# GpSimd's elementwise work goes to VectorE, and elu gets another instruction mix

## The chip, the cores and the metric

One NeuronCore of a Trainium2 chip runs the whole program. The metric is device time in microseconds (us) for one execution. Three runs of the kernel before gave 858.94, 859.1 and 861.25 us, so the median is 859.1 us.

Five engines work side by side, each through its own queue in program order: TensorE (PE, with its weight loads as PEld), VectorE (DVE), ScalarE (ACT), GpSimd (POOL) and SyncE (SP), which issues transfers. An instruction that waits holds up everything behind it on its engine.

## The reference, cut to what matters

```python
x = attn_out.transpose(0, 2, 1, 3).reshape(2304, 512)    # masked attention, 4 x 8 heads, 576 rows
order = argsort(-(x @ w_gate).flatten())                 # each token gets one of 8 experts,
...                                                      # each expert takes at most 288 tokens
for e in range(8):
    out[assigned == e] = np.maximum(x[assigned == e] @ w1[e], 0.0) @ w2[e]
h = out @ w_in                                           # 512 -> 2048
g = np.where(h > 0.0, h, np.exp(np.minimum(h, 0.0)) - 1.0)   # elu
return g @ w_out                                         # 2048 -> 512
```

All of it is float32. To keep that accuracy at TensorE's fast rate, each matmul operand is split into a high part (a rounded copy) and a low part (the rest), and each product is made of three matmuls: high by high, high by low, low by high.

## The kernel before, in words

The program has two stretches. Up to about 108 us it computes attention, 24 steps of a software pipeline. Behind it, for each of the eight experts in turn (`expert`, L1186), it computes the expert's two layers for 288 tokens (`h_item`, `y_item`), and then the dense layer pair for the full 128-token chunks that are ready (`hin_item`, `elu`, `out_item`; 256 or 384 columns, 16 slices of the 2048 hidden units). Beside this run the routing of a later expert (`Router.phase`: a chain of small DVE instructions with a group of small matmuls between them, six digit steps per expert), the gather of its rows (`rows_of`, indirect DMAs issued by POOL) and the splitting of the weights:

- Expert weights arrive as `raw` (128x512). `feeder` (L979) has ACT make the high part `wh` (L997) and then has a subtraction make the low part `wl` (L220, in `Dense.tt`). It runs on POOL or DVE.
- Dense weights arrive as 64-bit words, and `Dense.slice` (L229) unpacks them during attention and the first expert: two ACT instructions (L245, L248), a shift and two merges on DVE (L251, L256), two multiplications `g` and, for most slices, an ACT copy (L282) and two subtractions (`dense_lo`, `parts`). Multiplications and subtractions are L220 again, on POOL or DVE.

`Line` is a planner that runs while the program is built. It keeps an estimated clock for each engine and decides in which order the instructions are written; nothing of it runs on the chip. `Line.either` (L179) picks the engine for L220, and the flag `quiet` keeps POOL out:

```python
if self.free['pool'] <= self.now + POOL_AHEAD and not self.quiet:
    return 'pool'
if self.idle('dve', 65 + 1.05 * n):
    return 'dve'
```

Before, `quiet` is set only in the last digit step of the first routing (L715) and while gathers are outstanding (`rows_of`, L1032 to L1044).

`elu` (L1126) takes a PSUM tile `h` (in two cases the tile `yo` of another pool) with the dense layer's sums: ACT writes exp(h) to the SBUF tile `e` (L1146), DVE clamps it to 1 and subtracts 1 in place (L1148), DVE takes the maximum with `h` (L1150), ACT copies the result to the high part `ah` (L1152), and DVE makes the low part `al` by subtraction (L1154). For an expert's first layer the pair is ACT `ah` (L1082) and DVE `al` (L1084). PSUM tiles `h` have three buffers. TensorE waits for `al` and `wl` before the matmuls that read them.

Of the kernel before, what the change touches and what calls it, by code (L numbers as in the profile page):

```python
# [10 lines left out]
F32 = mybir.dt.float32  # L11
# [4 lines left out]
AF = mybir.ActivationFunctionType  # L16
OP = mybir.AluOpType
# [4 lines left out]
B, H, S, D = 4, 8, 576, 64  # L22
# [4 lines left out]
NS = len(BITS)  # L27
# [562 lines left out]
class Router:  # L590
# [100 lines left out]
    def phase(self, p, res, bank, then=None):  # L691


        nc, t, line, n = self.nc, {k: x[:, :self.n] if k in COLUMNS else x for k, x in self.t.items()}, self.line, self.n
        v, D = nc.vector, line.dve
# [7 lines left out]
        def pe(m, cost):  # L703
# [2 lines left out]
            line.now += m * cost  # L706
            return line.now + line.LAT

        if p:
            yield from self.prelude(p, 0, n)  # L710
        if p < 7:
            parts = ((0, n),) if p else ((0, 10), (10, 18))
            for i in range(NS):
                K = 2 ** BITS[i] - 1
                line.quiet = line.hush = p == 0 and i == NS - 1  # L715
                e = []
                for c0, c1 in parts:
                    n1 = self.against(t['ohU'][:, c0:c1, :K + 1], t['cur'][:, c0:c1], 96, 97 + K, OP.is_ge)
                    e.append(D(n1, fast=2) + line.late())
                if i == 0:  # L720
                    for j in range(1, NS):
                        self.digit(j, 0, n)
                    v.tensor_copy(t['digf'][:, 1:, :n], t['dig'][:, 1:, :n])
                    D(n * NS)
                else:
                    v.tensor_copy(t['di'], t['d'])
                    D(1)
                if i < NS - 1:
                    v.scalar_tensor_tensor(t['cd'], t['cur'][:, :, 0], 64.0, t['digf'][:, i + 1, :n], op0=OP.mult, op1=OP.add)
                    D(n)  # L730
                if i == 1:
                    v.tensor_scalar(t['pre'], t['di'], SHIFT[0], None, op0=OP.logical_shift_left)
                elif i > 1:
                    v.scalar_tensor_tensor(t['pre'], t['di'], SHIFT[i - 1], t['pre'], op0=OP.logical_shift_left, op1=OP.bitwise_xor)
                D(1)
                if i == 2:
                    v.tensor_scalar(t['mk'], t['pre'], 31, -1, op0=OP.arith_shift_right, op1=OP.bitwise_xor)
                    D(1)
                elif i == 3:
                    v.scalar_tensor_tensor(t['pre'], t['mk'], -2 ** 31, t['pre'], op0=OP.bitwise_or, op1=OP.bitwise_xor)  # L740
                    D(1)
                yield e[0]
                pc = yield from bank.take("pc")
                for (c0, c1), x in zip(parts, e):
                    yield x
                    for c in range(c0, c1):
                        nc.tensor.matmul(pc[:, :K], t['oh'][:, c, :], t['ohU'][:, c, :K], start=(c == 0), stop=(c == n - 1))
                yield pe(n, 30) if p else line.now + (c1 - c0) * 40 + line.LAT
                v.tensor_scalar(t['ok'][:, :K], pc[:, :K], CAP - 0.5, 0.0, op0=OP.is_ge, op1=OP.add, accum_out=t['d8'])
                e = D(K)  # L750
                bank.free(e + line.late())
                yield e
                v.transpose(t['tr'], t['d8'].to_broadcast([128, 32]))
                yield D(32)
                v.tensor_reduce(t['d'], t['tr'][:, 0:8], axis=AX.X, op=OP.max)
                e = D(8)
                if i == NS - 1:
                    v.tensor_reduce(t['di'], t['tr'][:, 0:8], axis=AX.X, op=OP.max)
                    D(8)
                yield e  # L760
                if i < NS - 1:
                    v.scalar_tensor_tensor(t['cur'], t['d'][:, :, None].to_broadcast([128, n, 4]), -64.0, bc(t['cd'], 4), op0=OP.mult, op1=OP.add)
                    e = D(4 * n)
                v.scalar_tensor_tensor(t['q'], t['tr'][:, 0:8], t['d'], t['q'] if i else self.e8, op0=OP.is_equal, op1=OP.mult)
                e = max(e, D(8))
                if i == NS - 1:
                    v.tensor_tensor(t['T'].bitcast(I32), t['di'], t['pre'], op=OP.bitwise_xor)
                    D(1)
                yield e
            eqe = t['q']  # L770
        else:
            eqe = t['eqe']
            v.scalar_tensor_tensor(eqe, self.caps, 0.0, self.e8, op0=OP.is_gt, op1=OP.mult)
            v.memset(t['T'], -2 * BIG)
            yield D(8)
# [7 lines left out]
        e = D(n)  # L783
        v.scalar_tensor_tensor(eqt, t['m'], t['T'], t['inE'], op0=OP.is_equal, op1=OP.mult)
        h = D(n) + line.late()
# [15 lines left out]
        e = D(2 * n)  # L801
# [7 lines left out]
        e = D(4 * n)  # L809
        v.tensor_tensor(t['V'], bc(t['t12'], 3), rb(self.io3, n), op=OP.is_equal)  # L810
        f = D(3 * n)
        yield e
        e = []
        for c0, c1 in parts if p < 7 else ((0, n),):
            n1 = self.against(t['ohU'][:, c0:c1, :96], t['u'][:, c0:c1], 0, 96, OP.is_equal)
            e.append(((c0, c1), D(n1, fast=2) + line.late()))
        (v if p else nc.gpsimd).tensor_tensor(
            t['vp'].rearrange("p c (v k) -> p c v k", k=4), t['V'][:, :, :, None].to_broadcast([128, n, 3, 4]),
            self.tokp[:, :, None, :].to_broadcast([128, n, 3, 4]), op=OP.mult)
        yield D(12 * n) + line.late() if p else line.pool(216, f)  # L820
        pi = yield from bank.take("pi")
        for (c0, c1), x in e:
            yield x
# [4 lines left out]
        e = D(12)  # L828
# [99 lines left out]
class Moe:  # L928
# [92 lines left out]
    def rows_of(self, p, res):  # L1021
        nc, line = self.nc, self.line
        while 'idx' not in res:
            yield line.now + 40
        idx = res['idx']
        rows = self.one.tile([96, 3, DM], F32, name="rows")
        at = []
        for v in range(3):
            nc.gpsimd.indirect_dma_start(out=rows[:, v], out_offset=None, in_=self.x_d[:, :],
                                         in_offset=bass.IndirectOffsetOnAxis(ap=idx[:, v, 0:1], axis=0))  # L1030
            at.append(line.dma(196608, line.put('pool', 1030), False) + GATHER)
        line.quiet = True  # L1032
        if p == 0:
            self.warm(WARM)
        nc.sync.dma_start(self.ids[CAP * p:CAP * p + CAP].rearrange("(v u) o -> u (v o)", u=96), idx[:, :, 1])
        if p:
            yield at[2]
            line.quiet = False
        while self.stage1 < p - 1:
            yield line.now + 60  # L1040
        for v in range(3):
            yield at[v] + (ROWS_LATE if p else 0)
            if not p and v == 2:
                line.quiet = line.hush = False  # L1044
            if p:
                pt = yield from self.bank.take("px")
            else:
                pt = self.hp.tile([128, 512], F32, name="h")
            pt = pt[:, 0:384].rearrange("p (k u) -> p k u", k=4)
            for k in range(4):  # L1050
                nc.tensor.transpose(pt[:, k], rows[:, v, 128 * k:128 * k + 128], self.identf[0:96, 0:96])
            line.now += 4 * 92
            h, l = self.xh[:, :, 96 * v:96 * v + 96], self.xl[:, :, 96 * v:96 * v + 96]
            yield line.now + line.LAT
            nc.scalar.activation(h, pt, AF.Copy)
            yield line.act(384)
            nc.vector.tensor_tensor(l, pt, h.bitcast(F32), op=OP.subtract)
            self.x_at = line.dve(384)
            if p:
                self.bank.free(self.x_at + line.late())  # L1060
        self.x_for = p
# [64 lines left out]
    def elu(self, ph, N, spare=None, split=False):  # L1126
        nc, line = self.nc, self.line
# [9 lines left out]
        def evac(c0, c1, E):  # L1137
            yield line.now + line.LAT
            if not E:
                while self.open == 2:  # L1140
                    yield line.now + 20
                self.open += 1
                E.append(self.tmp.tile([128, 384], F32, name="e")[:, :N])
            e, x, h, l = (z[:, c0:c1] for z in (E[0], ph, gh, gl))
            n = c1 - c0
            nc.scalar.activation(e, x, AF.Exp)  # L1146
            yield line.act(n)
            nc.vector.tensor_scalar(e, e, 1.0, -1.0, op0=OP.min, op1=OP.add)  # L1148
            line.dve(n, fast=2)
            nc.vector.tensor_tensor(e, e, x, op=OP.max)  # L1150
            yield line.dve(n)
            nc.scalar.activation(h, e, AF.Copy)  # L1152
            yield line.act(n)
            nc.vector.tensor_tensor(l, e, h.bitcast(F32), op=OP.subtract)  # L1154
            A['t'][c0 // 128:c1 // 128] = [line.dve(n)] * (n // 128)
            self.open -= c1 == N

# [214 lines left out]
```

## Time and profile before

| What | Value |
|---|---|
| median of three runs | 859.1 us (858.94 to 861.25) |
| the profiled execution's own time | 863.49 us |
| its span, first to last instruction | 861.7 us |
| PE busy | 755.2 us (88%) |
| DVE busy | 567.6 us (66%), 1591 instructions |
| ACT busy | 366.9 us (43%) |
| POOL busy | 317.8 us (37%) |
| mean granted TensorE clock | 0.941 |

Busy time counts an instruction from its start to its end, whatever it did in between; where an instruction was held up after it had started, the hold is in its busy time. Matmuls overlap, so a PE that is always busy need not be at its peak. The granted clock is given as a share: 1.00 is 2.4 GHz, 0.50 is 1.2 GHz.

### The profile page before, as it was taken

Reading aid. Unit: us, or ns where it says so; the run is one execution under the profiler, and the core shown is the slowest. Engines: PE = TensorE matmul, PEld = TensorE weight load, DVE = VectorE, ACT = ScalarE, POOL = GpSimd, SP = SyncE. Lnnn points to the kernel's source line nnn. Section 1 sums busy time; section 2 is a strip of 40 time slices with the busy share of each in tenths; the row PEclk is TensorE's granted clock in tenths of the full one; section 3 lists DMA queues with packets and bytes.
Section 4 is the critical chain, followed back from the end, with each engine's and each line's share of the span. In section 5 each row is a group of like instructions: output and inputs, shape, how many; then the busy total and the mean of one; then the engine's idle time right before and its main releaser. Section 6 shows DMA issues by size and latency. Waiting matters only on the chain. (4 is left out here: it accounts for less than half of the span.)

```text
span 861.7 us, 16868 instructions
## 1 busy us (share of the span) xinstructions
PE 755.2 (88%) x6300; PEld 681.7 (79%) x6300; DVE 567.6 (66%) x1591; ACT 366.9 (43%) x770; POOL 317.8 (37%) x257
## 2 busy tenths in 40 slices
PE   3987824889678989899989999899969999999997
PEld 2755523888568978898989889898969999999895
DVE  4977897999987776679667853566357425423331
ACT  2876822546524432353334323353334245344322
POOL 5143233863736430543164302640264153235101
PEclk9898955899979999999999999899999999999999
DMA  9999607767303360352034205420542432212000
GB/s 230 290 273 304 189 22 164 266 188 227 127 13 131 103 115 1 123 118 82 13 133 99 79 2 88 149 75 25 83 141 86 41 135 87 74 70 79 1 1 37
DMA packets 50658, 96.18 MB, mean 112 GB/s; under 512 B 10384, under 2 KB 20112, under 8 KB 48016
## 3 DMA queue, kind: packets, MB, share of 16 engines
q1 hardware_dynamic: 47600, 85.67, 33.2%
q0 software_dynamic: 2976, 9.44, 6.3%
q8 instruction: 49, 0.80, 0.4%
q14 instruction: 33, 0.27, 0.1%
HBM read 83.54 MB, written 11.54 MB: 110 GB/s over the span
## 5 line engine op out<-in xcount | busy, mean ns | idle before, releaser
L220 POOL TENSOR_TENSOR wl<-raw,wh 128x512 fp32r<-128x512 f32 x155 | 203.9, 1331 | 279.9 <-ACT wh L997 272.6
L997 ACT ACTIVATE wh<-raw 128x512 fp32r<-128x512 f32 x178 | 111.2, 629 | 143.5 <-PE h L956 60.6
L1148 DVE TENSOR_SCALAR e<-e 128x256 f32<-128x256 f32 (+2 forms) x138 | 58.5, 424 | 71.7 <-ACT e L1146 71.4
L1152 ACT ACTIVATE ah<-e 128x256 fp32r<-128x256 f32 (+2 forms) x135 | 56.8, 423 | 112.1 <-DVE e L1150 111.4
L1146 ACT ACTIVATE e<-h 128x256 f32<-128x256 f32 (+2 forms) x130 | 49.6, 389 | 115.9 <-PE h L956 113.4
L1154 DVE TENSOR_TENSOR al<-e,ah 128x256 fp32r<-128x256 f32 (+2 forms) x135 | 69.8, 523 | 35.0 <-ACT ah L1152 33.4
L956 PE MATMUL h<-yh,dense_lo 128*128 128x256 f32 (+1 forms) x284 | 85.3, 300 | 0.0
L956 PE MATMUL h<-yh,dense_hi 128*128 128x256 f32 (+1 forms) x284 | 85.0, 299 | 0.0
L956 PE MATMUL h<-yl,dense_hi 128*128 128x256 f32 (+1 forms) x284 | 85.0, 299 | 0.0
L956 PE MATMUL yo<-al,wh 128*128 128x288 f32 x256 | 79.1, 309 | 6.1 <-DVE al L1084 6.1
L956 PE MATMUL h<-xh,wl 128*128 128x288 f32 x256 | 77.0, 303 | 3.2 <-POOL wl L220 3.2
L956 PE MATMUL yo<-ah,wl 128*128 128x288 f32 x256 | 78.3, 306 | 1.4 <-POOL wl L220 1.4
L956 PE MATMUL yo<-ah,wh 128*128 128x288 f32 x256 | 78.3, 306 | 0.3 <-ACT ah L1082 0.3
L956 PE MATMUL h<-xh,wh 128*128 128x288 f32 x256 | 77.1, 304 | 0.0
L1084 DVE SCALAR_TENSOR_TENSOR al<-h,ah 128x288 fp32r<-128x288 f32 x64 | 29.0, 454 | 72.2 <-ACT ah L1082 72.0
L956 PE MATMUL h<-xl,wh 128*128 128x288 f32 x256 | 73.8, 302 | 0.0
L956 PE MATMUL yo<-dense_hi,al 128*128 128x512 f32 x156 | 62.9, 403 | 1.2 <-DVE al L1154 1.1
L220 POOL TENSOR_TENSOR g<-g,w 128x512 f32<-128x512 f32 x25 | 35.8, 1443 | 73.6 <-DVE g L256 26.6
L956 PE MATMUL yo<-dense_hi,ah 128*128 128x512 f32 x156 | 62.6, 401 | 0.0
L956 PE MATMUL yo<-dense_lo,ah 128*128 128x512 f32 x156 | 62.2, 398 | 0.0
L1180 POOL DMA_INDIRECT out<-orow,oi x18 | 17.7, 981 | 118.2 <-ACT orow L1178 85.7
L1150 DVE TENSOR_TENSOR e<-e,h 128x256 f32<-128x256 f32 (+2 forms) x130 | 56.1, 432 | 5.3
(239 smaller groups left out, 2007.0 us busy)
## 6 DMA issues: line engine op xcount, KB each, us to landing
raw<-in_we SPq DMA_DIRECT2D x128, 256.0 KB, 2.9
w<-in_wd SPq DMA_DIRECT2D x16, 1024.0 KB, 8.0
raw<-dense_words SPq DMA_DIRECT2D x52, 256.0 KB, 2.9
kd<-in_kt SPq DMA_DIRECT2D x16, 296.0 KB, 6.3
vd<-in_vb SPq DMA_DIRECT2D x16, 292.5 KB, 6.8
qt<-in_qt SPq DMA_DIRECT2D x8, 576.0 KB, 7.9
x_d<-os SPq DMA_DIRECT2D x32, 144.0 KB, 6.2
dense_words<-g SPq DMA_DIRECT2D x4, 512.0 KB, 2.9
```

Of the source, the lines that this page charges most:

```text
L220: (self.nc.vector if eng == 'dve' else self.nc.gpsimd).tensor_tensor(*a, **kw)
L956: self.nc.tensor.matmul(out, l, r, **kw)
L997: nc.scalar.activation(hi, r, AF.Copy)
L1084: nc.vector.scalar_tensor_tensor(al, ph, 0.0, ah.bitcast(F32), op0=OP.max, op1=OP.subtract)
L1146: nc.scalar.activation(e, x, AF.Exp)
L1148: nc.vector.tensor_scalar(e, e, 1.0, -1.0, op0=OP.min, op1=OP.add)
L1150: nc.vector.tensor_tensor(e, e, x, op=OP.max)
L1152: nc.scalar.activation(h, e, AF.Copy)
L1154: nc.vector.tensor_tensor(l, e, h.bitcast(F32), op=OP.subtract)
L1180: nc.gpsimd.indirect_dma_start(out=self.out[:, :], out_offset=bass.IndirectOffsetOnAxis(ap=oi[:, c:c + 1], axis=0), in_=t, in_offset=None)
```

## The change

Two edits stand in one diff. First, `quiet` becomes true when the first routing begins and is never reset, so that `either` returns only `'dve'` from there on; `r_vp` (L817), the one other elementwise instruction on POOL behind attention, goes to DVE too, and the planner's wait for the third gather is dropped. In the built program 181 instructions leave POOL for DVE: 155 `wl`, 25 of the dense weights' and `r_vp`. POOL keeps the gathers, the scatters of the output and its work during attention. Second, elu's clamp moves into ACT: relu(-h), then exp(-that), which is exp(min(h, 0)). One DVE instruction then adds -1, takes the maximum with `h` and writes it over `h` in PSUM; the high and low parts are made from there.

```diff
+        line.quiet = True
         if p:
             yield from self.prelude(p, 0, n)
...
-                line.quiet = line.hush = p == 0 and i == NS - 1
+                line.hush = p == 0 and i == NS - 1
...
-        (v if p else nc.gpsimd).tensor_tensor(
+        v.tensor_tensor(
             t['vp'].rearrange("p c (v k) -> p c v k", k=4), t['V'][:, :, :, None].to_broadcast([128, n, 3, 4]),
             self.tokp[:, :, None, :].to_broadcast([128, n, 3, 4]), op=OP.mult)
-        yield D(12 * n) + line.late() if p else line.pool(216, f)
+        yield D(12 * n) + line.late()
...
-        line.quiet = True
         if p == 0:
             self.warm(WARM)
...
-        if p:
-            yield at[2]
-            line.quiet = False
...
             if not p and v == 2:
-                line.quiet = line.hush = False
+                line.hush = False
...
-            nc.scalar.activation(e, x, AF.Exp)
+            nc.scalar.activation(e, x, AF.Relu, scale=-1.0)
+            line.act(n)
+            nc.scalar.activation(e, e, AF.Exp, scale=-1.0)
             yield line.act(n)
-            nc.vector.tensor_scalar(e, e, 1.0, -1.0, op0=OP.min, op1=OP.add)
-            line.dve(n, fast=2)
-            nc.vector.tensor_tensor(e, e, x, op=OP.max)
+            nc.vector.scalar_tensor_tensor(x, e, -1.0, x, op0=OP.add, op1=OP.max)
             yield line.dve(n)
-            nc.scalar.activation(h, e, AF.Copy)
+            nc.scalar.activation(h, x, AF.Copy)
             yield line.act(n)
-            nc.vector.tensor_tensor(l, e, h.bitcast(F32), op=OP.subtract)
+            nc.vector.tensor_tensor(l, x, h.bitcast(F32), op=OP.subtract)
```

In the rows below line numbers are those of each kernel; in the changed one L1079 is the ACT `ah` and L1081 the DVE `al` of an expert's first layer, L1143, L1145 and L1149 are ACT's relu, exp and copy of elu, and L1147 and L1151 DVE's maximum and subtraction.

The first place is DVE's queue in the first layer of the expert during which the planner starts the routing of expert 6 (its first instruction is `r_lm`). Before, two of the `wl` stand between the `al`, the others being on POOL:

```order
L220 TENSOR_TENSOR wl<-raw,wh 128x512
L1084 SCALAR_TENSOR_TENSOR al<-h,ah 128x288 x2
L220 TENSOR_TENSOR wl<-raw,wh 128x512
L1084 SCALAR_TENSOR_TENSOR al<-h,ah 128x288 x4
L655 TENSOR_TENSOR r_lm<-r_left,r_caps 128x72
L657 TENSOR_REDUCE r_m<-r_lm 128x9
```

In the changed kernel the same stretch reads:

```order
L1081 SCALAR_TENSOR_TENSOR al<-h,ah 128x288 x2
L220 TENSOR_TENSOR wl<-raw,wh 128x512 x3
L1081 SCALAR_TENSOR_TENSOR al<-h,ah 128x288
L220 TENSOR_TENSOR wl<-raw,wh 128x512 x2
L1081 SCALAR_TENSOR_TENSOR al<-h,ah 128x288
L220 TENSOR_TENSOR wl<-raw,wh 128x512 x2
L1081 SCALAR_TENSOR_TENSOR al<-h,ah 128x288
L220 TENSOR_TENSOR wl<-raw,wh 128x512 x2
L1081 SCALAR_TENSOR_TENSOR al<-h,ah 128x288
L220 TENSOR_TENSOR wl<-raw,wh 128x512
L655 TENSOR_TENSOR r_lm<-r_left,r_caps 128x72
```

About two `wl` now follow each `al` in DVE's queue.

The second place is DVE's queue in the first expert, where the second routing runs (`r_ok`, `r_tr`, `r_d` belong to a digit step). Before:

```order
L734 SCALAR_TENSOR_TENSOR r_pre<-r_di,r_pre 128x1
L740 SCALAR_TENSOR_TENSOR r_pre<-r_mk,r_pre 128x1
L1084 SCALAR_TENSOR_TENSOR al<-h,ah 128x288
L256 SCALAR_TENSOR_TENSOR g_2078<-w_1825,g_2078 128x512 x2
L749 TENSOR_SCALAR r_ok,r_d_96<-pc 128x31
L753 STREAM_TRANSPOSE r_tr<-r_d_96 128x32
```

In the changed kernel:

```order
L735 SCALAR_TENSOR_TENSOR r_pre<-r_di,r_pre 128x1
L741 SCALAR_TENSOR_TENSOR r_pre<-r_mk,r_pre 128x1
L1081 SCALAR_TENSOR_TENSOR al<-h,ah 128x288
L220 TENSOR_TENSOR wl<-raw,wh 128x512 x2
L750 TENSOR_SCALAR r_ok,r_d_96<-pc 128x31
L754 STREAM_TRANSPOSE r_tr<-r_d_96 128x32
```

Here `wl` stands where a merge of dense weights stood, which comes later now. From the second routing's first instruction to the last `parts`, DVE's queue held 14 of the L220 before and holds 61 now, 47 more, and 14 elu pieces lose their L1148. On PE the matmuls of that routing's ranking (`pb`) stood behind 152 of the experts' matmuls and stand behind 102 now.

## Rows read from the trace of the kernel before

**Rows 1.** Windows: busy time of each engine in two stretches (us), clock, DMA.
```profile
core 0: us, PE busy (x) PEld busy (x) DVE busy (x) ACT busy (x) POOL busy (x), PEclk, DMA share, GB/s
143.80:245.40 101.60, 77.75 (x591) 70.95 (x592) 96.82 (x205) 53.06 (x98) 61.61 (x44) 0.87 0.59 190
245.40:852.00 606.60, 583.05 (x4138) 541.87 (x4137) 358.08 (x1076) 233.09 (x537) 203.08 (x165) 0.98 0.29 76
```

**Rows 2.** Timeline from 195 to 204 us, DVE: start, duration, instruction.
```profile
197.16 0.69 DVE L251 TENSOR_SCALAR g<-g 128x1024 uint32<-128x1024 uint32 x1
197.76 0.28 DVE L1148 TENSOR_SCALAR e<-e 128x256 f32<-128x256 f32 x1
198.08 0.42 DVE L1150 TENSOR_TENSOR e<-e,h 128x256 f32<-128x256 f32 x1
198.42 0.42 DVE L1154 TENSOR_TENSOR al<-e,ah 128x256 fp32r<-128x256 f32 x1
198.76 0.69 DVE L256 SCALAR_TENSOR_TENSOR g<-w,g 128x512 uint32<-128x512 uint32 x1
...
201.50 1.29 DVE L220 TENSOR_TENSOR wl<-raw,wh 128x512 fp32r<-128x512 f32 x2
```

**Rows 3.** Timeline around 352 to 360 us, POOL, DVE and PE.
```profile
351.92 6.25 POOL L220 TENSOR_TENSOR wl<-raw,wh 128x512 fp32r<-128x512 f32 x5
...
352.16 6.04 DVE L764 SCALAR_TENSOR_TENSOR r_q<-r_tr,r_d,r_q 128x8 f32<-128x8 f32 x1
...
359.18 0.24 DVE L784 SCALAR_TENSOR_TENSOR r_ge<-r_m,r_T,r_inE 128x18 bf16<-128x18 f32 x1
...
359.46 0.18 PE L795 MATMUL pb<-r_ge,r_tri 128*128 128x36 bf16 x1 [3.29 <-DVE r_ge L784]
```

**Rows 4.** Groups by form, DVE, 143.8 to 245.4 us: count, busy us, mean ns.
```profile
L256 DVE SCALAR_TENSOR_TENSOR g<-w,g 128x512 uint32<-128x512 uint32 x17 | 14.2, 856 | 0.1
L1154 DVE TENSOR_TENSOR al<-e,ah 128x256 fp32r<-128x256 f32 x12 | 9.5, 788 | 0.5 <-ACT ah L1152 0.5
L1148 DVE TENSOR_SCALAR e<-e 128x256 f32<-128x256 f32 x12 | 9.3, 777 | 0.7 <-ACT e L1146 0.7
L251 DVE TENSOR_SCALAR g<-g 128x1024 uint32<-128x1024 uint32 x8 | 7.7, 964 | 0.0
...
L220 DVE TENSOR_TENSOR g<-g,w 128x512 f32<-128x512 f32 x5 | 6.2, 1236 | 0.1
...
L764 DVE SCALAR_TENSOR_TENSOR r_q<-r_tr,r_d,r_q 128x8 f32<-128x8 f32 x5 | 4.3, 857 | 0.0
L220 DVE TENSOR_TENSOR parts<-g,parts 128x512 fp32r<-128x512 f32 x3 | 4.1, 1399 | 0.0
L729 DVE SCALAR_TENSOR_TENSOR r_cd<-r_cur,r_digf 128x18 f32<-128x18 bf16 x5 | 3.9, 780 | 0.0
...
L784 DVE SCALAR_TENSOR_TENSOR r_ge<-r_m,r_T,r_inE 128x18 bf16<-128x18 f32 x1 | 1.3, 1304 | 0.0
```

**Rows 5.** Waits of PE, 245.4 to 860 us: total us, times, longest.
```profile
PE yo L956 <- DVE al L1084: 6.1, 2, 3.1
PE pc L747 <- DVE r_ohU L619: 5.6, 2, 3.0
PE pb L795 <- DVE r_ge L784: 3.3, 1, 3.3
PE px L1051 <- DMA rows<-x_d,r_iall: 2.8, 1, 2.8
PE h L956 <- POOL wl L220: 2.4, 1, 2.4
```

**Rows 6.** Windows: four stretches behind such waits, and their sum.
```profile
360.90:364.30 3.40, 3.40 (x16) 3.40 (x15) 2.60 (x4) 1.35 (x3) 1.95 (x2) 0.50 0.47 157
...
sum 17.00, PE 16.05 PEld 16.02 DVE 12.64 ACT 4.55 POOL 2.95; mean PE 4.01 PEld 4.00 DVE 3.16 ACT 1.14 POOL 0.74
```

**Rows 7.** Waits of DVE over the whole span.
```profile
DVE wl L220 <- ACT wh L997: 18.3, 12, 3.6
```

## The prediction

> **What bounds the kernel now.** I read the windows first, because the shares for the whole run mix two very different stretches. From 143.8 to 245.4 us (the first expert, with the unpacking of the dense weights; I call it stage A) DVE is busy for 96.8 of 101.6 us while PE has work for only 77.8 [rows 1]. DVE sets the pace there. From 245.4 to 852 us (stage B) PE is busy for 583 of 606.6 us, and DVE for 358 [rows 1]. PE sets the pace there, and time can only come from the 23.6 us in which PE idles and from stretches at half clock.
>
> The timeline then shows what DVE's busy time consists of. At 197.76 us the clamp L1148 of a 128x256 piece takes 0.28 us, the subtraction L1154 0.42 us, the shift L251 and the merge L256 0.69 us each [rows 2]. In stage A as a whole the same four groups have means of 777, 788, 964 and 856 ns [rows 4]. The reader should ask what stretches an instruction of fixed size. The timeline at 352 us answers it: POOL starts five `wl` in a row at 351.92 us, 6.25 us in all, and a DVE instruction on eight elements per partition that starts at 352.16 us ends only at 358.2 us, as POOL does. The instruction that PE waits for, L784, comes some 6 us late, and PE stands still for 3.29 us [rows 3]. So DVE is held while POOL computes, and the hold is hidden in DVE's busy time. The maximum L1150, which reads PSUM, took 0.42 us where I looked, while its neighbours that read only SBUF grew.
>
> There are five such bursts in stage B, at 266.8, 351.9, 436.0, 541.6 and 629.8 us, one for each of five experts. They are what I hold behind PE's main waits there: `al` 6.1 us, `r_ohU` 5.6 us, `r_ge` 3.3 us, and `wl` itself 2.4 us [rows 5].
>
> **The change part by part.** *Stage A, the holds go.* I take each group's mean in stage A less its undisturbed duration [rows 2 to 4]: L256 17 x 0.17 = 2.8 us; L1154 12 x 0.37 = 4.4; L1148 12 x 0.50 = 6.0; L251 8 x 0.27 = 2.2; `g` 5 x 0.55 = 2.7 and `parts` 3 x 0.71 = 2.1, both against the 0.69 of an equal size; for the routing's small ones, against 0.24, L764 5 x 0.62 = 3.1 and L729 5 x 0.54 = 2.7; five single instructions like L784 5 x 1.06 = 5.3. The sum is 31 us. Smaller groups, left out, would add to it.
>
> *Stage A, the work comes.* In the built order 47 more of the L220 stand in DVE's queue in this stage. Two in a row take 1.29 us and the last of them 0.69, so each occupies DVE for 0.60 us [rows 2]: 28.2 us. Fourteen clamps leave, 0.32 us each from start to start [rows 2], at most 4.4 us. DVE's need becomes 101.6 - 31 + 28.2 - 4.4 = 94.4 us, its idle time included. PE needs 77.8, so DVE still decides: **7.2 us less**. The bounds are 0, if new waits fill what is freed, and 16 us, if the holds left out and DVE's 4.8 us of idle time go too; PE's own 77.8 us and its half clock (mean 0.87 [rows 1]) forbid much more.
>
> *elu.* The new maximum has one PSUM input as L1150 has, and writes PSUM, which no DVE row here does. Below, it costs the 0.42 us of L1150; above, I bound it by the 0.69 us of the dearest equal-type instruction, L256 on twice the columns [rows 2], which would add 14 x 0.27 = 3.8 us in stage A and nothing in stage B, where DVE has 248 us free. I take 0.42. ACT gets one instruction more for each piece. Even at 0.69 us, 14 of them are 10 us on an engine that is busy for 53 of 101.6 us [rows 1]; PE asks for a piece's `al` only two slices later in the code, which covers a longer chain. In stage B nothing else covers it: if that lead were gone, each of some 120 pieces could cost its extra link of about 0.4 us, 48 us.
>
> The Trainium skill's page Perfetto Trace Analysis, in the section Optimizing Scalar/DVE Operations, gives DVE about 60 ns of access overhead on SBUF and about 125 ns on PSUM, so by the page the in-place maximum would be up to 65 ns dearer, and the estimate for stage A 0.9 us higher. The trace shows no such difference: L1150, with a PSUM input, and L1154, without one, both take 0.42 us [rows 2].
>
> *Stage B, the holds go.* The waits on `al`, `r_ohU`, `r_ge` and `wl` sum to 17.4 us [rows 5]. Four stretches at half clock follow such waits: 17.0 us with 16.05 us of PE work at 0.50 [rows 6], which takes 8.0 us at full clock. Together 25.4 us. Not all of it goes. The `wl` of a burst still have to be made, now by DVE, at 0.60 instead of 1.25 us each, and two stand behind each `al`. I take a fifth back, because a burst of five costs DVE 3 us instead of holding it for 6, and because it is spread between the `al` instead of standing ahead of them: **20.3 us less**. The bounds are 10 and 25.4. Next in line is then the wait for the gathered rows, 2.8 us [rows 5], which this leaves alone. POOL's queue holds only gathers and scatters, which can go earlier, but nothing shows PE waiting for them to be issued.
>
> *The first routing, 108 to 139 us.* Some holds go there as well, but `r_vp` moves from POOL, where it ran beside DVE, into DVE's chain, and a `wl` now stands ahead of the instruction that makes the row indices. I take 0, between -2 and +2.
>
> The sum is 7.2 + 20.3 + 0 = 27.5 us. The profiled execution took 863.49 us and would take 836; it stands 4.4 us over the median, so I carry the difference over: 859.1 - 27.5 = **831.6 us**.
>
> **The rivals.** *1. A new wait takes the old one's place.* In stage A the second routing's matmuls stand further ahead in PE's queue (behind 102 instead of 152 matmuls), so PE may meet them before DVE has made their operands and stand still with the experts' matmuls behind them. Then stage A gives nothing and stage B half, 13 us: 846 us. For it speaks that DVE remains the bound; against it, that DVE's chain gets shorter too.
>
> *2. Nothing is left.* The holds go, but the 0.60 us pieces delay `al` in small amounts, each too short to see. It needs about 27 us over 155 `wl`, 0.18 us each, and would end near 859.
>
> *3. Slower: DVE waits in place for the cast.* POOL could wait for ACT's `wh` with nothing behind it; on DVE everything stands behind. The 23 `wl` that DVE already makes waited for ACT for 18.3 us [rows 7], 0.8 us each, so 155 more would wait for 123 us. DVE has 248 us free in stage B [rows 1], and ACT holds `ah` behind the same cast, so most of it should coincide with waits that exist. It decides once 27.5 of the 123 us, 22%, land on PE. With a third the time is 859.1 - 27.5 + 41 = 873 us.
>
> *4. Slower: the long durations are not POOL's doing.* Then stage A pays 28.2 - 4.4 us and loses nothing, so DVE's bound grows by 24 us, to 883 us. Rows 3 and the undisturbed pairs in rows 2 speak against it. The same section of the Trainium skill says that with DVE saturated, moving work off it, even to GpSimd, may make sense, though the two share a port; this change goes the opposite way where DVE is busy for 95% of a stage, and by that rule the time would be this rival's.
>
> *5. More than forecast.* Stage A reaches its 16 us and stage B its 25.4: 818 us, or a few less if the first routing gains its 2.
>
> **How the numbers follow.** Forecast 0.60 (its own range 820 to 843), rival 1 0.16, rival 2 0.05, rival 3 0.08, rival 4 0.03, rival 5 0.08. A difference within 0.3%, 2.6 us, cannot be told from none; the three runs lie within 2.3 us. Faster is the forecast and rivals 1 and 5, 0.84; the same 0.05; slower 0.11. For eight in ten I go down to 814, which takes in rival 5, and up to 852, which takes in rival 1 and leaves out rivals 2 to 4 and a little more.
>
> **What would show it.** In the changed profile, stage A's groups of rows 4 must fall to the durations of rows 2, and no DVE instruction on a few elements may last over a microsecond. DVE must still be busy for most of that stage, which must be some 7 us shorter. In stage B PE's waits for `al`, `r_ohU` and `r_ge` of 3 us must be gone, and the half clock behind them. Wrong it would be if PE's list of waits led with `wl` from DVE, if DVE's waits for `wh` rose towards 100 us with PE idle beside them, or if elu's maximum in PSUM took far over 0.42 us.

## The result, and the profile after

| | before | changed | ratio, 95% interval |
|---|---|---|---|
| median of four runs | 859.02 us (858.67 to 861.25) | 833.51 us (830.21 to 836.09) | 0.9696 [0.9649, 0.9742] |
| the profiled execution, its own time | 863.49 us | 835.83 us | |
| its span | 861.7 us | 834.1 us | |

The change takes 25.5 us off, and 831.6 us were forecast. That the two agree says little yet: the prediction had one term for each stretch, and these have to be compared one by one. I cut both executions at the same three instructions: attention's last matmul, the first matmul of the first expert and the first of the second expert. Stage A runs between the last two, stage B from there to PE's last matmul. (The prediction's borders, 143.8 and 245.4 us, were instructions of DVE's routing chain, which the change moves.)

Windows of the kernel before at these borders: length, busy time of each engine with its instruction count, granted clock, DMA share, GB/s.

```profile
102.40:152.40 50.00, 19.80 (x247) 14.65 (x237) 40.96 (x163) 13.73 (x21) 15.68 (x13) 0.59 0.49 124
...
152.40:254.20 101.80, 82.26 (x593) 75.00 (x591) 95.06 (x200) 51.72 (x98) 60.34 (x44) 0.90 0.53 167
254.20:855.10 600.90, 577.35 (x4104) 536.61 (x4103) 351.95 (x1050) 231.16 (x532) 204.04 (x166) 0.98 0.29 77
```

And of the changed kernel:

```profile
core 0: us, PE busy (x) PEld busy (x) DVE busy (x) ACT busy (x) POOL busy (x), PEclk, DMA share, GB/s
104.50:149.70 45.20, 18.48 (x247) 13.90 (x237) 33.13 (x166) 9.09 (x16) 3.02 (x3) 0.65 0.42 103
...
149.70:252.40 102.70, 85.25 (x594) 76.19 (x592) 87.22 (x229) 62.75 (x119) 3.25 (x3) 0.89 0.54 180
252.40:827.50 575.10, 568.65 (x4105) 528.76 (x4103) 326.89 (x1059) 277.11 (x653) 36.17 (x35) 1.00 0.30 81
```

Read the third number of each line, its length. Attention ends 2.1 us later, the first routing is 4.8 us shorter (forecast 0, at most 2), stage A is **0.9 us longer** (forecast 7.2 shorter), and stage B is 25.8 us shorter (forecast 20.3). Behind PE's last matmul both have 6.6 us. The sum is -27.6 us, the difference of the two spans. So a term that failed outright was covered by two that were too small, and that the sum came within 0.1 us of the forecast is luck. The DVE column shows how: in stage A DVE's busy time fell by 7.8 us, about as forecast, and yet the stage got no shorter, because DVE now idles for 15.5 us in it where it idled for 6.7. In stage B the gain is where it was forecast: PE's idle time fell by 17.1 us and its busy time by 8.7 us, for which the forecast had 17.4 and 8.0.

The groups that answer to [rows 4], DVE in the changed kernel's stage A (count, busy us, mean ns, idle before):

```profile
L220 DVE TENSOR_TENSOR wl<-raw,wh 128x512 fp32r<-128x512 f32 x28 | 18.5, 682 | 1.2 <-ACT wh L998 1.2
L220 DVE TENSOR_TENSOR g<-g,w 128x512 f32<-128x512 f32 x20 | 13.5, 684 | 0.0
L256 DVE SCALAR_TENSOR_TENSOR g<-w,g 128x512 uint32<-128x512 uint32 x18 | 11.9, 686 | 0.1
L251 DVE TENSOR_SCALAR g<-g 128x1024 uint32<-128x1024 uint32 x9 | 6.2, 687 | 0.1
...
L1151 DVE TENSOR_TENSOR al<-h,ah 128x256 fp32r<-128x256 f32 x13 | 5.4, 416 | 0.0
L220 DVE TENSOR_TENSOR dense_lo<-g,dense_hi 128x512 fp32r<-128x512 f32 x7 | 4.6, 683 | 0.0
L220 DVE TENSOR_TENSOR parts<-g,parts 128x512 fp32r<-128x512 f32 x6 | 4.0, 688 | 1.3 <-ACT parts L282 1.3
...
L765 DVE SCALAR_TENSOR_TENSOR r_q<-r_tr,r_d,r_q 128x8 f32<-128x8 f32 x5 | 1.1, 221 | 0.0
```

Means of 964, 856, 788 and 857 ns are now 687, 686, 416 and 221: the holds are gone.

The same view over the whole run, for elu's maximum in PSUM:

```profile
L220 DVE TENSOR_TENSOR wl<-raw,wh 128x512 fp32r<-128x512 f32 x178 | 121.8, 689 | 74.0 <-ACT wh L998 73.1
L1147 DVE SCALAR_TENSOR_TENSOR h<-e,h 128x256 f32<-128x256 f32 x84 | 35.9, 427 | 49.2 <-ACT e L1145 48.7
L1151 DVE TENSOR_TENSOR al<-h,ah 128x256 fp32r<-128x256 f32 x84 | 35.1, 418 | 13.0 <-ACT ah L1149 12.3
L1081 DVE SCALAR_TENSOR_TENSOR al<-h,ah 128x288 fp32r<-128x288 f32 x64 | 28.9, 451 | 8.8 <-ACT ah L1079 8.8
```

The maximum takes 0.427 us, where I took 0.42. DVE waited 73.1 us for `wh`, which was rival 3's mechanism. Whether PE paid for it is in PE's waits. In stage B these are all of them (total us, times, longest):

```profile
PE px L1048 <- DMA rows<-x_d,r_iall: 5.5, 2, 4.1
PE yo L957 <- DVE al L1081: 0.8, 1, 0.8
```

The waits on `al`, `r_ohU`, `r_ge` and `wl` [rows 5] shrank to 0.8 us; the wait for gathered rows is next in line, as forecast, and grew from 2.8 to 5.5. The stage's granted clock is 1.00 instead of 0.98. In stage A PE's list begins otherwise:

```profile
PE h L957 <- DVE wl L220: 6.9, 7, 1.5
PE h L957 <- ACT parts L282: 5.0, 2, 4.2
```

A list led by `wl` from DVE was one of the prediction's signs of being wrong, and in stage A it came true. It is not rival 3's wait, though: ahead of the 28 `wl` of this stage DVE idled for `wh` for only 1.2 us (first line of its groups above).

So the question that the result leaves is stage A: where did the 7.2 us go?

### The profile page after: what moved, and what is told of

It is laid out like the page before. It is cut to its first block, busy times and chain, and to the rows that moved or that the text cites. A ratio compares the mean times of both kernels' runs of the same rounds, so it can differ in the third digit from the quotient of the medians.

```text
span 834.1 us, 16709 instructions
## 1 busy us (share of the span) xinstructions
PE 746.6 (90%) x6300; PEld 673.9 (81%) x6300; DVE 526.0 (63%) x1634; ACT 419.2 (50%) x908; POOL 80.5 (10%) x76
## 5 line engine op out<-in xcount | busy, mean ns | idle before, releaser
L220 DVE TENSOR_TENSOR wl<-raw,wh 128x512 fp32r<-128x512 f32 x178 | 121.8, 689 | 74.0 <-ACT wh L998 73.1
L1147 DVE SCALAR_TENSOR_TENSOR h<-e,h 128x256 f32<-128x256 f32 (+2 forms) x130 | 56.8, 438 | 105.2 <-ACT e L1145 85.0
L1143 ACT ACTIVATE e<-h 128x256 f32<-128x256 f32 (+2 forms) x130 | 50.6, 389 | 117.5 <-PE h L957 117.1
L957 PE MATMUL yo<-al,wh 128*128 128x288 f32 x256 | 76.0, 297 | 0.8 <-DVE al L1081 0.8
L957 PE MATMUL yo<-ah,wh 128*128 128x288 f32 x256 | 75.5, 295 | 0.0
L1149 ACT ACTIVATE ah<-h 128x256 fp32r<-128x256 f32 (+2 forms) x127 | 48.0, 385 | 35.3 <-DVE h L1147 35.0
L1151 DVE TENSOR_TENSOR al<-h,ah 128x256 fp32r<-128x256 f32 (+2 forms) x127 | 53.0, 425 | 19.4 <-ACT ah L1149 18.6
L1145 ACT ACTIVATE e<-e 128x256 f32<-128x256 f32 (+2 forms) x138 | 59.0, 428 | 4.4
L957 PEld LDWEIGHTS h<-yh,dense_hi 128*128 128x128 f32 x284 | 54.7, 193 | 4.2 <-ACT dense_hi L282 2.2
L957 PEld LDWEIGHTS h<-yh,dense_lo 128*128 128x128 f32 x284 | 54.7, 193 | 2.9 <-DVE dense_lo L220 1.0
L957 PEld LDWEIGHTS h<-xh,wl 128*128 128x128 f32 x256 | 49.3, 193 | 7.5 <-DVE wl L220 6.7
```

The lines of the kernel that those rows point to most:

```text
L220: (self.nc.vector if eng == 'dve' else self.nc.gpsimd).tensor_tensor(*a, **kw)
L957: self.nc.tensor.matmul(out, l, r, **kw)
L1143: nc.scalar.activation(e, x, AF.Relu, scale=-1.0)
L1145: nc.scalar.activation(e, e, AF.Exp, scale=-1.0)
L1147: nc.vector.scalar_tensor_tensor(x, e, -1.0, x, op0=OP.add, op1=OP.max)
L1149: nc.scalar.activation(h, x, AF.Copy)
```

## The experiments

The runs are of several chips, on which the kernel before took 859 to 868 us, so each run is compared, as a ratio, with the kernel before run beside it on its chip. In the profiled executions attention's last matmul came at anything from 100.2 us (e4) to 108.7 us (e3), although the order is the same up to there; therefore stages are compared by their lengths. All times of stages are from windows like those above, and each is of one execution. Two of the changed kernel (changed and e10 in the table) differ by 1.6 us in stage A and 1.5 us in stage B, so differences of that size are not read; the one of the kernel before was 4.5 us over its median.

| run | ratio, 95% interval | stage A, us | stage B, us |
|---|---|---|---|
| before | 1 | 101.8 | 600.9 |
| changed | 0.9696 [0.9649, 0.9742] | 102.7 | 575.1 |
| e1_pool_part | 0.9756 [0.9722, 0.9789] | 112.0 | 575.6 |
| e2_elu_part | 0.991 [0.9879, 0.994] | 96.8 | 603.0 |
| e3_pool_in_first | 0.9706 [0.9668, 0.9744] | 94.9 | 578.0 |
| e4_dense_first | 0.9764 [0.9711, 0.9816] | 101.7 | 573.9 |
| e5_pool_copy_work | 1.0655 [1.0595, 1.0716] | 122.1 | 643.6 |
| e6_pool_memsets | 0.9862 [0.9802, 0.9922] | 104.7 | 593.0 |
| e7_pool_first_expert | 0.9671 [0.9627, 0.9716] | 97.9 | 575.1 |
| e8_pool_dense_only | 0.9747 [0.9701, 0.9794] | 97.4 | 572.7 |
| e9_order_kept | 0.9571 [0.9526, 0.9616] | 90.0 | 578.1 |
| e10_after_again | 0.9701 [0.9653, 0.9749] | 101.1 | 573.6 |
| e11_before_on_dve | 0.9479 [0.9449, 0.951] | 89.7 | 572.8 |
| e12_before_on_dve_elu | 0.9509 [0.9466, 0.9553] | 89.0 | 573.3 |

### Each half of the change alone

*e1_pool_part* is the changed kernel with the old elu. *e2_elu_part* is the kernel before with the new elu, POOL computing as before.

```diff
# e1: the changed kernel, elu's hunk taken back
-            nc.scalar.activation(e, x, AF.Relu, scale=-1.0)
-            line.act(n)
-            nc.scalar.activation(e, e, AF.Exp, scale=-1.0)
+            nc.scalar.activation(e, x, AF.Exp)
...
-            nc.vector.scalar_tensor_tensor(x, e, -1.0, x, op0=OP.add, op1=OP.max)
+            nc.vector.tensor_scalar(e, e, 1.0, -1.0, op0=OP.min, op1=OP.add)
+            line.dve(n, fast=2)
+            nc.vector.tensor_tensor(e, e, x, op=OP.max)
...
# e2: the kernel before, and of the change only elu's hunk
```

> The changed kernel with the old elu (exp, clamp and maximum on an SBUF tile), so only the POOL part of the change. Theory: the gain comes from POOL no longer holding DVE in the five bursts behind 245 us, so nearly all of it stays: 834 to 839 us, no DVE instruction on a few elements over 1 us, PE's 3 us waits on al, r_ohU and r_ge absent. Rival, the elu part carries the gain: 850 us or more.

> The kernel before with the new elu, POOL's arithmetic as it was. Theory: the five bursts still hold DVE (instructions of 5 us and more on a few elements), so little is gained: 853 to 859 us. Rival, the elu part carries the gain: 833 to 842 us.

Windows of stage A and stage B, first e1:

```profile
152.50:264.50 112.00, 87.11 (x594) 78.14 (x592) 92.32 (x248) 57.38 (x102) 3.25 (x3) 0.86 0.52 165
264.50:840.10 575.60, 568.80 (x4104) 528.66 (x4103) 358.75 (x1179) 232.51 (x532) 35.24 (x35) 1.00 0.31 81
```

And e2:

```profile
150.30:247.10 96.80, 81.73 (x594) 75.25 (x592) 86.45 (x178) 58.19 (x115) 57.82 (x42) 0.90 0.57 183
247.10:850.10 603.00, 579.71 (x4104) 538.62 (x4103) 299.37 (x937) 276.75 (x653) 204.50 (x165) 0.97 0.30 77
```

Stage B belongs to POOL's part alone: 575.6 with it, 603.0 without. In stage A the halves pull apart. Elu's part takes 5.0 us off (the forecast had 4.4), and POOL's part costs 10.2 us, where the forecast had 28.2 - 31 = 2.8 us less. So the term that failed is POOL's part in stage A. (The profiled execution of e1 was 3.3 us over its median, so the 10.2 may be too high by some of that.) The expectations were in microseconds of the first chip. By their ratios e1 would take 838 us there, as expected, and e2 851 us, a little less than the 853 to 859 expected.

### Does the late unpacking bound stage A?

In the changed kernel the loads of the dense words are issued later. SP's queue from 140 us on, before and then changed, the first two loads each:

```profile
144.33 0.38 SPq L237 DMA_DIRECT2D w<-in_wd  x1
147.77 0.50 SPq L237 DMA_DIRECT2D w<-in_wd  x1
```

```profile
164.47 0.43 SPq L237 DMA_DIRECT2D w<-in_wd  x1
...
186.81 0.43 SPq L237 DMA_DIRECT2D w<-in_wd  x1
```

*e3_pool_in_first* lets POOL compute until the dense weights are unpacked, in the first routing too. *e4_dense_first* keeps POOL out and lets the planner serve the unpacking earlier in its turn.

```diff
# e3: the changed kernel
-        line.quiet = True
         if p:
...
                 line.finish(*work)
+                line.quiet = True
                 dense.keep()
# e4: the changed kernel
-        work = [line.add(dense.worker(k), 2) for k in range(WORKERS)]
+        work = [line.add(dense.worker(k), 1) for k in range(WORKERS)]
```

> The changed kernel with POOL allowed to compute again until the dense weights are unpacked (first expert), none behind that. The predicted step for the first expert (without POOL it is 7 us shorter) says that this costs 7 us: 840 us. The theory formed from the changed kernel's trace (that stage gained nothing, because the unpacking is written and loaded 20 us later) says the same time or a little less: 829 to 835 us, with the stage from the first expert's first matmul to the second's at 99 to 103 us.

> The changed kernel with the planner's dense-weight workers moved from level 2 to level 1, ahead of the expert weights' feeder and the later routing: the word loads stand behind 6, 6 and 15 raw loads in SP's queue instead of 13, 16 and 18. Theory, the first expert's stage is bound by the late start of the unpacking: the stage falls from 102.7 us to 93 to 98, the time to 824 to 829 us. Rival, ACT is the bound of that stage (18 of 20 us busy at 200 to 220 us) or DVE's total work is: the stage stays at 101 to 104 us, the time at 831 to 836.

e3's stage A takes 94.9 us, less than the 99 to 103 expected, and it is shorter with POOL where the prediction's step would have it 7 us longer. But its first routing takes 51.5 where the changed kernel takes 45.2:

```profile
108.70:160.20 51.50, 19.85 (x249) 14.57 (x237) 42.57 (x165) 13.48 (x21) 18.29 (x15) 0.60 0.50 125
160.20:255.10 94.90, 80.79 (x592) 73.70 (x590) 83.93 (x175) 58.06 (x114) 57.51 (x40) 0.89 0.57 177
```

Most of what it wins in one stretch it loses in the other, and its ratio is that of the changed kernel. e4's stage A takes 101.7 us, where 93 to 98 were expected. Its first routing takes 56.4 us, with PE waiting 11.8 us for the first expert's rows instead of 6.7, so that it is no faster as a whole. An earlier turn for the unpacking alone is not what stage A lacks. That left two readings: DVE has too much to do in stage A, or the order as a whole is worse.

### Order or work

*e7_pool_first_expert* admits POOL only from the first expert's gathered rows until the unpacking is done. *e8_pool_dense_only* is e7 with every `wl` on DVE. *e9_order_kept* is planned like e7, so that PE, ACT and SP hold the same instructions in the same order, but what the planner gave to POOL in the first expert is executed by DVE at the place where it is written. *e10_after_again* is the changed kernel, beside them on the same chip.

```diff
# e7: the changed kernel
-        line.quiet = True
+        line.quiet = line.quiet or not p
...
-                line.hush = False
+                line.quiet = line.hush = False
...
                 line.finish(*work)
+                line.quiet = True
                 dense.keep()
# e8: e7, in feeder
-                e = yield from line.either(512)
-                t = dense.tt(e, 512, lo, r, hi.bitcast(F32), op=OP.subtract)
+                yield from line.room('dve', 603)
+                t = dense.tt('dve', 512, lo, r, hi.bitcast(F32), op=OP.subtract)
# e9: e7
...
-        (self.nc.vector if eng == 'dve' else self.nc.gpsimd).tensor_tensor(*a, **kw)
+        (self.nc.vector if eng == 'dve' or self.swap else self.nc.gpsimd).tensor_tensor(*a, **kw)
...
-                line.quiet = line.hush = False
+                line.quiet, line.hush, self.dense.swap = False, False, True
```

> The changed kernel, but POOL may take subtractions and multiplications from the gathers of the first expert until the dense weights are unpacked. The first routing and everything behind the first expert stay as in the changed kernel. By both theories the first expert takes about 95 us from its first matmul to the next expert's (96.8 and 94.9 us in the two runs that had POOL there, 102.7 us in the changed kernel), and the first routing stays at about 45 us behind attention's last matmul: 6 to 8 us less than the changed kernel, a ratio to the kernel before of 0.960 to 0.963.

> As e7_pool_first_expert, but in the first expert POOL may take only the dense weights' multiplications and subtractions; every wl is DVE's. Theory order (DVE idles early because the dense unpacking is written late, and the first expert ends with it): the dense work gets written as early as in the kernel before, so the first expert takes 95 to 98 us. Rival work (DVE has too much to do in the first expert): half of the relief, 98 to 101 us.

> The order of e7_pool_first_expert on PE, ACT and SP, to the instruction, but the L220 that the planner gave to POOL in the first expert are executed by DVE at the place where they are written. Theory order: DVE's busy time is then about 87 us and its idle time that of the kernel before, 7 us: the first expert takes 94 to 97 us, as with POOL. Rival work: DVE cannot take it on, the first expert takes 102 us or more, as in the changed kernel.

> The changed kernel itself, beside the three others on the same chip: a ratio of 0.970 to the kernel before by both theories, the first expert 102 to 103 us. It says what e7 to e9 are to be compared with.

Windows of e9, the first 20 us of stage A:

```profile
147.50:167.50 20.00, 20.00 (x191) 19.70 (x189) 19.58 (x67) 12.38 (x20) 0.00 (x0) 0.95 0.57 205
...
147.50:237.50 90.00, 80.56 (x595) 72.53 (x593) 81.98 (x219) 60.05 (x117) 2.82 (x3) 0.93 0.63 204
```

And of e10, the same two stretches:

```profile
150.40:170.40 20.00, 17.15 (x172) 16.16 (x170) 14.89 (x64) 8.38 (x15) 0.00 (x0) 0.90 0.41 146
...
150.40:251.50 101.10, 82.85 (x594) 74.03 (x592) 87.39 (x229) 62.88 (x119) 3.25 (x3) 0.91 0.56 183
```

This decides it. In both runs DVE does all the arithmetic; only the planner's belief about one stage differs, and the stage takes 90.0 or 101.1 us; the intervals of the two timed ratios do not touch. In e9's first 20 us DVE is busy for 19.58 us and PE for 20.00; in e10 for 14.89 and 17.15, and over the whole stage A of e10 PE waits 7.0 us for `wl`, which in e9's it never does. The reading that DVE has too much to do is refuted, and e9's 90.0 us are even less than the 94 to 97 expected. ACT, named as a rival bound with e4, has nearly the same work in both (60.05 and 62.88 us). Part of the gain is lost behind: e9's stage B is 4.5 us longer than e10's, with PE busy for 2.6 us more and waiting 1.9 us more for gathered rows; why is not shown. e7 against e9 is the price of POOL's help at one and the same order, holds and slower pieces together: 97.9 against 90.0 us, 7.9 us. e7 missed its expectation: its stage A is 3 us shorter than e10's, not 6 to 8, and the intervals of the two overlap. e10 itself came out as expected by its ratio, its stage A 1 us shorter. e8's stage A, 97.4 us, lies in the range expected of the order (95 to 98) but only 0.6 us below that of the work (98 to 101), so it does not part them. Its first routing took 51.9 us where e10's took 46.1, nearly all of it in PE's wait for the first expert's rows (12.3 us instead of 6.8), and it is no faster than e10.

The Trainium skill, on the page Perfetto Trace Analysis, section Optimizing Scalar/DVE Operations, says that with DVE saturated some work may be moved off it, even to GpSimd, and warns that the two share a port so that this might not help. Here the warning holds: in e7, with DVE busy for 88.96 of the stage's 97.9 us, GpSimd's help cost 7.9 us against e9.

### The whole exchange at the order before

*e11_before_on_dve* is the kernel before, with its own elu and its planner untouched. PE, ACT and SP hold exactly its order; what stood on POOL behind attention, `r_vp` too, is executed by DVE. *e12_before_on_dve_elu* adds the new elu, that is, it is to e2 what e11 is to the kernel before.

```diff
# e11: the kernel before; e12: the same on e2
...
-        (self.nc.vector if eng == 'dve' else self.nc.gpsimd).tensor_tensor(*a, **kw)
+        (self.nc.vector if eng == 'dve' or self.line.swap else self.nc.gpsimd).tensor_tensor(*a, **kw)
...
+        line.swap = True
         if p:
             yield from self.prelude(p, 0, n)
...
-        (v if p else nc.gpsimd).tensor_tensor(
+        v.tensor_tensor(
```

> The kernel before, with its elu and with the order of PE, ACT and SP as before, but from the first routing on every elementwise instruction that stood on POOL is executed by DVE where it is written. Theory order: at a kept order the exchange of holds for work gives a little in the first expert (31 us of holds against 28.2 us of work), so that takes 97 to 100 us, where the same work in the planner's new order took 112.0 us; behind it the 25 us of the kernel with only POOL's part (575 to 578 us). A ratio of 0.960 to 0.967. Rival work: the first expert takes 108 us or more whatever the order. Rival planner: behind the first expert a planner that does not know where the work is done writes the al too late, and 585 us or more are needed there.

> As e11_before_on_dve, with the new elu. Theory order: the first expert takes 88 to 91 us, as in e9_order_kept, and the stretch behind it 574 to 578 us; a ratio of 0.953 to 0.960, equal to e9_order_kept. Rival planner: the first expert as well, but 585 us or more behind it, a ratio of 0.968 or more.

Windows of e11:

```profile
150.20:239.90 89.70, 78.13 (x594) 71.14 (x592) 83.91 (x238) 52.65 (x98) 3.63 (x3) 0.93 0.59 192
239.90:812.70 572.80, 568.89 (x4105) 529.79 (x4103) 360.17 (x1181) 232.21 (x532) 35.17 (x35) 0.99 0.31 81
```

And of e12:

```profile
156.20:245.20 89.00, 78.96 (x595) 71.92 (x593) 79.28 (x218) 58.00 (x115) 3.11 (x3) 0.93 0.61 193
245.20:818.50 573.30, 567.96 (x4104) 528.97 (x4103) 327.16 (x1063) 277.09 (x653) 36.23 (x35) 1.00 0.30 81
```

e11 is the fastest kernel of this study: 821.01 us beside 866.68 for the kernel before, a ratio of 0.9479 whose interval [0.9449, 0.951] lies wholly below that of the changed kernel run again [0.9653, 0.9749]. It beat its expectation of 0.960 to 0.967, by stage A above all (89.7 us, where 97 to 100 were expected). The planner need not know who computes: behind the first expert its old order needs 572.8 us, so the rival by which 585 us or more are needed is refuted. e12's stage A, 89.0 us, is in the expected range, its stage B and its ratio are a little below theirs. Its interval overlaps that of e11; at this order elu's new mix is worth nothing that these runs can tell.

### Is it POOL's arithmetic that holds DVE?

*e5_pool_copy_work*: the changed kernel, and POOL makes each `wl` a second time into a tile that nobody reads. *e6_pool_memsets*: instead POOL copies one column of `wh` into that tile, as a release, and then fills the tile with zeros three times. Both add work; nothing is left out.

```diff
+        self.extra = self.one.tile([128, 512], F32, name="extra")
...
# e5, behind ACT's wh
+                nc.gpsimd.tensor_tensor(self.extra, r, hi.bitcast(F32), op=OP.subtract)
# e6, at the same place
+                nc.gpsimd.tensor_copy(self.extra[:, 0:1], hi[:, 0:1].bitcast(F32))
+                for _ in range(3):
+                    nc.gpsimd.memset(self.extra, 0.0)
```

> The changed kernel in which POOL makes every low part of the raw weights a second time, into a scratch tile that nothing reads (178 subtractions more on POOL, reading raw and wh as before; DVE's work and order are untouched). Theory, POOL's arithmetic holds DVE: DVE instructions with two SBUF inputs stretch to a multiple again, and the time goes back to 850 to 875 us. Rival, the gain came from where the low parts are made (an earlier wl, a lighter POOL queue): 833 to 838 us, since nobody waits for the scratch tile but the raw buffers.

> The changed kernel in which POOL, for every raw weight, copies one column of wh into a scratch tile and sets the tile to 0 three times: POOL is busy about as long, but reads next to nothing from SBUF. If any POOL arithmetic holds DVE, the time goes back as with the second subtraction, to 850 us or more. If it is POOL's reads that hold it, as the Trainium skill's page SBUF - State Buffer, section Who interferes with whom, says of a DVE instruction with two SBUF inputs, wl and al keep 0.69 and 0.42 us and the time stays at 832 to 840 us.

Groups by form of DVE in e5, the whole run:

```profile
L220 DVE TENSOR_TENSOR wl<-raw,wh 128x512 fp32r<-128x512 f32 x178 | 177.8, 1005 | 67.2 <-ACT wh L999 66.4 <-issue 0.2
L1149 DVE SCALAR_TENSOR_TENSOR h<-e,h 128x256 f32<-128x256 f32 x84 | 35.7, 425 | 40.5 <-ACT e L1147 40.1
...
L1083 DVE SCALAR_TENSOR_TENSOR al<-h,ah 128x288 fp32r<-128x288 f32 x64 | 28.7, 449 | 8.0 <-ACT ah L1081 8.0
```

And in e6, POOL first, then DVE:

```profile
L1005 POOL MEMSET extra<- 128x512 f32 x540 | 286.2, 530 | 31.4
...
L220 DVE TENSOR_TENSOR wl<-raw,wh 128x512 fp32r<-128x512 f32 x178 | 122.0, 690 | 88.9 <-ACT wh L999 87.8
```

With POOL's subtractions beside it `wl` takes 1005 ns on DVE instead of 689, 56 us in all; with 286 us of memsets it takes 690. So POOL's arithmetic holds DVE, and its memsets do not. In e5 itself the instructions with one input in PSUM, L1149 and L1083, keep their 425 and 449 ns (427 and 451 in the changed kernel). The Trainium skill's page SBUF — State Buffer, section Who interferes with whom, states both rules: a DVE instruction with two SBUF inputs contends with a GpSimd instruction that reads SBUF, not with one that only writes it, and one with a single SBUF input outside the two-port modes does not contend. The rows agree. A single input in SBUF does not by itself keep an instruction free of holds, however: L1148 and L251 have just one, and were held before (777 and 964 ns [rows 4]); whether they ran in a two-port mode no run here shows.

The times missed their expectations. e5, 923.21 us, is slower even than the kernel before, where 850 to 875 us were expected. e6, 856.28 us, is slower than the 832 to 840 expected, and than the changed kernel, by 0.9862 to 0.9701. In e6 that is another mechanism, in ACT's waits in its stage B (total us, times, longest):

```profile
ACT wh L999 <- POOL extra L1003: 26.6, 17, 8.0
ACT wh L999 <- POOL extra L1005: 20.3, 19, 3.1
```

ACT waited 46.9 us for buffers of `wh` that POOL had still to read, and what ACT makes behind them came late: PE waited 7.6 us there for ACT's `ah`, which in the changed kernel it never did, and was busy for 8.4 us longer at a granted clock of 0.98 instead of 1.00. That is most of the 17.9 us by which its stage B is longer. How much of e5's loss is of this kind was not separated.

## Why the prediction was right, and which step failed

**What bounds the kernel.** Right on holds: e5, e6 and the durations after the change show it. (Two of the five bursts were longer than five `wl`: 11 from 541.58 us, and 10 that began at 627.35 us.) Right that PE sets the pace in stage B. For stage A, "DVE still decides" is the step that failed.

**Stage A, forecast -7.2, measured +0.9.** The prices were sound. DVE's busy time fell by 7.8 us, and 61 of the L220 stand in the stage (28, 20, 7 and 6 in the groups above), as the order said. But six of the 47 that came are not work that POOL did in this stage: at the order before, e11, 41 come. At that kept order the exchange gives more than I forecast: in e11 DVE is busy for 11.2 us less with 38 instructions more, which at the forecast's 0.60 us each makes an estimated 34 us of holds where I had counted 31 and left the small groups out, and the stage is 12.1 us shorter. What failed is the step from DVE's need to the stage's length, which kept the idle time as it was. `either` writes an L220 for POOL as soon as POOL is about to be free; with `quiet` it writes it only when its estimate has DVE free, so the dense slices come later (the second load above at 186.81 us instead of 147.77), and DVE stands idle early in the stage (busy for 14.89 of the first 20 us in e10). I had the order in hand and read from it how many instructions moved, not what each engine would find ready. That new order costs 11.1 us (e10 against e9). Which piece of it costs most stays open; e4 shows only that an earlier turn for the unpacking is not enough.

**elu.** Its 4.4 us fit the order before (5.0, e2), its 0.42 us hold, and the longer chain cost little or nothing in stage B (603.0 against 600.9 in e2, 573.3 against 572.8 in e12). But its worth hangs on the rest: 10.9 us of stage A in the planner's new order (e1 against e10, single executions; the timed ratios, 0.9756 and 0.9701, show about half of that, and their intervals overlap), about nothing once the holds are gone and the order is kept (e11 against e12).

**Stage B, forecast -20.3, measured -25.8.** The sum of waits and half clock, 25.4 us, was right; the fifth taken back was not. With two `wl` behind each `al`, PE's waits for `al` come to 0.8 us in the whole stage.

**The first routing, forecast 0, measured -4.8.** POOL's busy time falls from 15.68 to 3.02 us and DVE's from 40.96 to 33.13. Holds are only a part of that: at the order before, with all of POOL's arithmetic there on DVE, the stretch takes 48.5 us in e11 and 49.5 in e12, which is inside my bound of 2. In the new order 6 of the L220 stand in it instead of 13, while stage A holds six more than in e11 (61 against 55), five of them of the dense weights. So work was moved from this stretch into stage A, and the forecast had no term for that.

**The rivals.** Rival 1 had stage A right in size (nothing) and wrong in cause: no wait of PE on the routing is in its list there. And it had stage B at half, 13 us, where 25.8 came. Rival 3's waits came at half the price, 73.1 us for 178 `wl`, 0.41 us each, and PE's list for stage B has no wait on `wl`. Rivals 2 and 4 are refuted by the times and by e5. Rival 5's 25.4 us of stage B came, its stage A did not.

## What to carry to other kernels

Moving work to another engine under a planner is two changes, a new price and a new order of everything; measure the first alone by letting the planner keep its old belief (e11), since here the order took back 11 us that the price had earned. Here an instruction of fixed size whose mean lay well over its smallest duration was being held by another engine: look for such groups, and count the holds at that difference, the small instructions too. And when a total agrees with its forecast, compare it stretch by stretch before believing the reasons, and look for work that has moved from one stretch to the next.

## What the runs showed of the hardware that was not expected

In e5 POOL and DVE work on the same kind of subtraction, and each `wl` of DVE loses 316 ns on average, while the instructions with an input in PSUM lose nothing. And in e6 286 us of memsets beside DVE added 1 ns to `wl`. So in these runs POOL's busy time did not tell what its work cost DVE; what POOL read, and where DVE's own operands lay, did.

The same attention, with the same order, ended between 100.2 and 108.7 us in the profiled executions. No run here explains it; it is larger than most effects in the table, and only the lengths of stages and the timed ratios could be compared.
